# w_in's third block behind the casts, batch 1's globals ahead of w_out, batch 0's gathers ahead of the iotas

## Chip, cores and metric

The kernel runs on 1 core of one Trainium2 chip. The metric is the time of one execution in device microseconds, as the median of several runs; lower is better. Before the change it is 374.94 us, the median of 3 runs (374.66 to 376.61).

The core's engines work side by side, each through its own list of instructions in order: PE (matrix multiply), DVE (vector), ACT (activation functions), POOL (general, and the issuer of every transfer that casts or gathers) and SP (issuer of the plain transfers and of the transposing ones). They wait for one another by semaphores.

## What is computed

Attention with a band of 32 positions to each side and 8 global positions, for 8 batches of 8 heads, 576 positions and 64 values per head; then, on the 4608 tokens of 512 values, two matrix products with a periodic activation between them. Inputs and output are float32.

```
scores = scale * q @ k.T          # scale = 1/sqrt(64)
mask   = |i - j| <= 32  or  i is global  or  j is global
scores = where(mask, scores, -1e9)
attn   = softmax(scores)
x      = (attn @ v)  as [tokens, heads * 64]
h = x @ w_in                      # 512 x 2048
g = h + sin(alpha * h)**2 / (alpha + 1e-9)
out = g @ w_out                   # 2048 x 512
```

## The kernel before

The order of work on every engine is written out by hand. Attention of batch b+1 runs together with the second product (`gemm2`) of batch b, and then `gemm1` of batch b+1 follows; `gemm2`'s matmuls are dealt out by `fill(n)`, n at a time, between the others. All of PE's work is one list in program order, so a matmul that waits holds back all that stand behind it.

**Attention.** For each batch the keys lie in KX, the queries in QX, the values in VX (two buffers of each, by b % 2), each cut into blocks of 48 positions with the 8 global ones beside them, so that one 128-wide product covers both. A head pair hp (four per batch) has three groups of `scores` (L741), each followed on ACT by an exp (L749) and on DVE by a product with MASK (L752). `products` (L783) then multiply E by VX (key 0) and by OB, for the sums (key 1); for batch 1 and later those of head pair hp - 1 are done in the turn of hp. Logarithm, exponential and product give the normalised rows xT (L809 to L815).

**gemm1(b).** 16 groups nt of 8 matmuls each (L990), into PSUM banks named n, r, d and o (`order`): o is the pair zo, which is also gemm2's and, once, that of `turn_kq`. Each group is read by ACT (sine, L1020), squared on ACT or DVE (L1024, L1026), and put together on DVE into H (L1028). Groups 0 to 3 use columns of w_in's first block, 4 to 7 of the second, 8 to 11 of the third, 12 to 15 of the fourth. During groups 10 to 13 of batch 0, DVE also places half of batch 1's keys and queries (`place`, L349 and L356).

**Transfers.** POOL issues `load_w_in` (four blocks, L410), `load_w_out` (four blocks, L416), `load_v` (L393, four transfers per head pair), `cast_qk` (L330, a batch's k and q cast to bf16 in DRAM), and the indirect gathers of batch 0's global rows (L553). SP issues `turn_qk` (L339, the transposing loads kt and qt of cast k and q), `gather` (L488, eight transfers each: the global rows of all batches, gk, gq and gv) and `load_vg` (L402, the global rows of v into VX). After its three memsets for batch 1's buffers POOL waits, by a copy into `seen` (L1118), until kt has landed; only behind that stand w_in's third and fourth block, the values of batch 1's head pairs 0 and 1, and, on SP behind qt, `gather(v, gv)`.

**Globals.** `turn_kq` (L697) turns gk and gq by eight PE transposes into zo[1] and copies them on DVE to kTg and qTg. `cast_globals_v` (L695) casts gv to VGb on POOL. `place_globals(b)` (L366) copies kTg and qTg on POOL into KX and QX of a batch: eight copies of 64x96 and two of 128x112. Batch 0's own globals come earlier, from the three gathers at L553 (g0k, g0q, VG0).

**The start.** POOL issues batch 0's k and q (four loads, L443), makes the identity and six iotas (qrel four times, qpos, jrow), then the three gathers. ACT clears QX and half of VX, squares qrel (L557), clears the rest of VX. DVE makes `band` and MASK from qrel, then `far` from qpos and the global positions (L638 to L666), which it puts into MASK. PE turns keys and queries (`turn_part`, L590); ACT places the first keys (`place_part`, L606), DVE the first queries (L611), and ACT the globals of batch 0 (L621, L630).

In `gemm1`, at group 11 of batch 0, the order before is:

```
            if b == 0 and nt == 11:
                turn_kq()
            if b == 0 and nt == 11:

                load_w_out()
                cast_globals_v()
                place_globals(1)
                load_v(1, (2, 3))
                load_vg(1)
```

Of the kernel before, what the change touches and what calls it, by code (L numbers as in the profile page):

```python
# [247 lines left out]
def kernel(  # L248
# [117 lines left out]
    def place_globals(b):  # L366

        for hp in range(NHP):
            for t in range(2):
                rows = slice(t * D, (t + 1) * D)  # L370
                nc.gpsimd.tensor_copy(
                    out=KX[b % 2][rows, hp, :, t * D + KT : t * D + KT + NG],
                    in_=kTg[rows, hp, None, :, b].to_broadcast([D, NT12, NG]),
                )
# [73 lines left out]
    qrel = setup.tile([P, 2, 2, WCOL // 2], DT.float32, name="qrel")  # L448
    for par, left in ((0, PAD), (1, 40)):
        nc.gpsimd.iota(qrel[:, par, :, 0:left], pattern=[[1, 2], [2, left]], base=-WIN,  # L450
                       channel_multiplier=0, allow_small_or_imprecise_dtypes=True)
        nc.gpsimd.iota(qrel[:, par, :, left:60], pattern=[[1, 2], [2, 60 - left]],
                       base=2 * left - 40, channel_multiplier=0, allow_small_or_imprecise_dtypes=True)
    qpos = setup.tile([P, NT12, 2, 24], DT.float32, name="qpos")
    nc.gpsimd.iota(qpos[:], pattern=[[KT, NT12], [1, 2], [2, 24]], base=0, channel_multiplier=0,
                   allow_small_or_imprecise_dtypes=True)
    jrow = setup.tile([P, NG], DT.float32, name="jrow")
    nc.gpsimd.iota(jrow[:], pattern=[[1, NG]], base=0, channel_multiplier=0,
                   allow_small_or_imprecise_dtypes=True)


# [71 lines left out]
    nc.vector.tensor_copy(out=grow[:], in_=rowf[0 : NG * B, 4:5])  # L533
    nc.vector.memset(kflat[:, half : 2 * half], 0.0)
# [15 lines left out]
    g0 = {}  # L550
    for name, src in (("k", k), ("q", q), ("v", v)):
        g0[name] = VG0 if name == "v" else setup.tile([NG * B, D], DT.bfloat16, name="g0" + name)
        nc.gpsimd.indirect_dma_start(  # L553
            out=g0[name][:], out_offset=None, in_=src[0].rearrange("h s d -> (h s) d"),
            in_offset=bass.IndirectOffsetOnAxis(ap=grow[:, 0:1], axis=0),
        )
    nc.scalar.activation(out=qrel[:], in_=qrel[:], func=AF.Square, bias=kpos[:, 0:1], scale=-1.0)  # L557
    clear(vflat[:, half : 2 * half])
# [5 lines left out]
    cast_qk(1)  # L564
    load_vg(0)
# [62 lines left out]
    def place_global_queries(t, copy):  # L628
# [7 lines left out]

    gpf = setup.tile([P, 1], DT.float32, name="gpf")
    nc.vector.tensor_copy(out=gpf[:], in_=gp64[:].bitcast(DT.int32)[:, 0:1])  # L638
    nc.scalar.activation(out=qpos[:], in_=qpos[:], func=AF.Square, bias=gpf[:, 0:1], scale=-1.0)
# [6 lines left out]
    later = setup.tile([P, NG], DT.float32, name="later")  # L646
    nc.vector.tensor_scalar(
        out=later[:], in0=jrow[:], scalar1=pm, scalar2=float(-KT), op0=ALU.subtract, op1=ALU.is_ge
    )
# [3 lines left out]
    nc.vector.scalar_tensor_tensor(  # L653
        out=cond[:, 2:3], in0=pm, scalar=float(KT + NG - 1), in1=cond[:, 1:2], op0=ALU.is_le, op1=ALU.mult
    )
    nc.vector.tensor_tensor(out=fone[:], in0=fone[:], in1=cond[:, 2:3], op=ALU.mult)

    far = setup.tile([P, NT12, 2, 24], DT.bfloat16, name="far")
    nc.vector.tensor_scalar(
        out=far[:], in0=qpos[:], scalar1=float(WIN * WIN) + 0.5,  # L660
        scalar2=fone[:, 0:1], op0=ALU.is_gt, op1=ALU.mult,
    )
    farv = far[:].rearrange("p (t e) x c -> p t e x c", e=2)
    for e, c0 in ((0, 20), (1, 16)):
        own = M2[:, :, e].rearrange("p t (x c) -> p t x c", x=2)[:, :, :, c0 : c0 + 24]
        nc.vector.tensor_tensor(out=own, in0=own, in1=farv[:, :, e], op=ALU.max)  # L666

    turn_part(1, 0, views([zn[:, n, :] for n in range(2)]))
    for n in range(2):
        place_part(1, 0, n, act)  # L670
# [542 lines left out]
```

## Time and profile before

| | us |
|---|---|
| median of 3 runs | 374.94 |
| the profiled execution | 374.3 |
| its span, first to last instruction | 372.6 |
| PE busy in the span | 338.7 |
| ACT busy | 293.9 |
| DVE busy | 282.8 |
| POOL busy | 138.3 |
| attention of batch 0: first scores on PE | 15.48 |
| gemm1 of batch 0: first matmul | 31.97 |
| attention of batch 1: first scores | 54.05 |
| gemm1 of batch 1: first matmul | 71.67 |

The profile is of one execution; its times are measured from the span's start. In a timeline each line has the start, the time taken (several like instructions merged, "xN"), the engine, the line of the kernel, the operation, output and inputs by their names in the program, shapes and types, and in brackets the idle time of the engine just before it with what ended it. The name H stands for several tiles that lie in one buffer, among them gk, gq and gv. Transfers issued by POOL run in one queue (q0, software), those of SP in another (q1, hardware); both are carried out by the same 16 DMA engines. The time of a transfer "to landing" counts from its issue.

### The profile page before, as it was taken

The numbers are of one execution on the slowest core, as the hardware profiler recorded it, in microseconds if no ns is written. First come the engines' busy times: TensorE is split into PE (matmuls) and PEld (weight loads), VectorE is DVE, ScalarE is ACT, GpSimd is POOL, SyncE is SP. The second block draws the span as 40 slices with busy tenths as digits, with TensorE's granted clock in tenths as the row PEclk, the third lists the DMA queues.
The fourth block names the chain that finished last, engine by engine and source line by source line (L and its number), as shares of the span: only waits on it lengthen the run. The fifth ranks groups of instructions, "written<-read, shape, count | busy, mean of one in ns | idle before, by whom it ended". The sixth has DMA issues, their size and how long they took to land. (4 is left out here: it accounts for less than half of the span.)

```text
span 372.6 us, 8428 instructions
## 1 busy us (share of the span) xinstructions
PE 338.7 (91%) x3040; PEld 228.7 (61%) x3040; DVE 282.8 (76%) x621; ACT 293.9 (79%) x566; POOL 138.3 (37%) x246
## 2 busy tenths in 40 slices
PE   1678769999998999999999999999999999994993
PEld 1567546766576766767676756776667666551441
DVE  6777897598878787888788878888878776888240
ACT  7799897888878788878888888888888988788110
POOL 7894596669844604470357016700000000000001
PEclk9999998999999999999999999999999999998998
DMA  6999999999999586966498517626100000101211
GB/s 120 115 158 209 152 155 184 147 186 187 154 210 213 35 157 100 160 98 90 68 175 119 84 58 67 65 46 143 30 28 30 23 35 31 31 0 35 75 61 52
DMA packets 103579, 38.07 MB, mean 102 GB/s; under 512 B 94138, under 2 KB 98250, under 8 KB 103082
## 3 DMA queue, kind: packets, MB, share of 16 engines
q0 software_dynamic: 56640, 18.56, 43.9%
q1 hardware_dynamic: 46890, 18.89, 24.4%
q8 instruction: 26, 0.43, 0.5%
q14 instruction: 23, 0.19, 0.2%
HBM read 37.15 MB, written 17.83 MB: 148 GB/s over the span
## 5 line engine op out<-in xcount | busy, mean ns | idle before, releaser
L1047 PE MATMUL zo<-w_out,H 128*128 128x512 bf16 x576 | 155.4, 382 | 4.9 <-ACT osb L1053 4.9
L990 PEld LDWEIGHTS <-w_in 128*128 128x128 bf16 x1024 | 98.6, 98 | 47.7 <-issue 10.3
L393 POOL DMA_DIRECT2D VX<-in_v_dram x128 | 83.2, 662 | 92.7 <-PE zd L783 60.9
L1047 PEld LDWEIGHTS <-H 128*128 128x128 bf16 x576 | 52.6, 98 | 43.4 <-issue 7.2
L749 ACT ACTIVATE E<-ring 128x480 bf16<-128x480 f32 x96 | 54.3, 568 | 21.8 <-PE ring L741 21.4
L752 DVE TENSOR_TENSOR E<-E,MASK 128x480 bf16<-128x480 bf16 x96 | 35.9, 404 | 16.8 <-ACT E L749 15.5
L1075 POOL DMA_INDIRECT out_dram<-osb,grow x1 | 1.0, 998 | 126.9 <-DVEq L1181 126.9
L1028 DVE SCALAR_TENSOR_TENSOR H<-s,recipT,zn 128x576 bf16<-128x576 bf16 x47 | 38.2, 813 | 10.0 <-ACT s L1024 6.2
L1024 ACT ACTIVATE s<-sb 128x576 bf16<-128x576 bf16 (+1 forms) x62 | 42.7, 689 | 2.0
L1020 ACT ACTIVATE sb<-zn,alphaT 128x576 bf16<-128x576 f32 (+1 forms) x47 | 34.8, 740 | 11.6 <-PE zn L990 11.6
L741 PE MATMUL ring<-QX,KX 128*128 128x120 bf16 x384 | 37.8, 224 | 6.3 <-ACT E L749 3.3
L741 PEld LDWEIGHTS <-KX 128*128 128x128 bf16 x384 | 28.8, 101 | 21.9 <-issue 10.3
L1028 DVE SCALAR_TENSOR_TENSOR H<-s,recipT,zd 128x576 bf16<-128x576 bf16 x39 | 31.7, 813 | 6.6 <-ACT s L1024 4.7
L1028 DVE SCALAR_TENSOR_TENSOR H<-s,recipT,zr 128x576 bf16<-128x576 bf16 x39 | 31.7, 812 | 4.6 <-ACT s L1024 2.5
L1053 ACT COPY osb<-zo 128x512 f32<-128x512 f32 x36 | 20.7, 578 | 17.8 <-PE zo L1047 14.8
L1026 DVE TENSOR_TENSOR s<-sb 128x576 bf16<-128x576 bf16 (+1 forms) x66 | 30.6, 464 | 5.2 <-ACT sb L1020 4.9
L1020 ACT ACTIVATE sb<-zd,alphaT 128x576 bf16<-128x576 f32 (+1 forms) x39 | 28.9, 741 | 7.2 <-PE zd L990 5.6
L1020 ACT ACTIVATE sb<-zr,alphaT 128x576 bf16<-128x576 f32 (+1 forms) x39 | 28.9, 741 | 5.6 <-PE zr L990 5.6
L783 PEld LDWEIGHTS <-VX 128*128 128x128 bf16 x448 | 26.3, 99 | 9.3 <-issue 3.1
L990 PE MATMUL zn<-xT,w_in 128*128 128x288 bf16 x184 | 26.9, 286 | 4.2 <-DMA w_in<-in_moe_w_in_dram 2.0
L990 PE MATMUL zn<-xlast,w_in 128*128 128x288 bf16 (+1 forms) x192 | 28.8, 289 | 0.3
L783 PE MATMUL zn<-E,VX 128*128 128x120 bf16 (+2 forms) x336 | 26.6, 210 | 1.0 <-DVE xlast L815 0.9
(159 smaller groups left out, 488.3 us busy)
## 6 DMA issues: line engine op xcount, KB each, us to landing
VX<-in_v_dram POOLq DMA_DIRECT2D x128, 36.0 KB, 5.6
kd<-in_k_dram POOLq DMA_DIRECT2D x7, 576.0 KB, 7.2
qd<-in_q_dram POOLq DMA_DIRECT2D x7, 576.0 KB, 9.2
w_in<-in_moe_w_in_dram POOLq DMA_DIRECT2D x4, 512.0 KB, 6.5
w_out<-in_moe_w_out_dram POOLq DMA_DIRECT2D x4, 512.0 KB, 8.9
out_dram<-osb SPq DMA_DIRECT2D x8, 256.0 KB
out_dram<-osb SPq DMA_DIRECT2D x8, 224.0 KB
out_dram<-osb SPq DMA_DIRECT2D x8, 192.0 KB
```

Source lines behind the costliest of these rows:

```text
L393: nc.gpsimd.dma_start(out=VX[b % 2][r : r + 24, hp, :, t * D : t * D + D], in_=v[b, 2 * hp + t].rearrange("(i a y) d -> y a i d", a=24, y= ...
L741: nc.tensor.matmul(out=ps[:, e * WCOL : (e + 1) * WCOL], lhsT=kx[:, hp, i, :], rhs=qx[:, hp, :, s0 : s0 + 60], start=True, stop=True, skip ...
L749: nc.scalar.activation(out=Eg, in_=ps[:, 0 : 4 * WCOL], func=AF.Exp, scale=scale, accum_out=EA[:, n : n + 1])
L752: nc.vector.tensor_tensor(out=Eg, in0=Eg, in1=MASK[:, 4 * g : 4 * g + 4, :].rearrange("p i c -> p (i c)"), op=ALU.mult,)
L783: nc.tensor.matmul(out=out_t[:, half, :, a - half * CUT : z - half * CUT], lhsT=OB[:] if key else VXb[:, hp, i, :], rhs=E[:, i, :, a - s0 ...
L990: nc.tensor.matmul(out=h[e][:, 0:W], lhsT=lhsT, rhs=xT[:, c, e, 0:W], start=(c == 0), stop=(c == CT - 1), skip_group_check=True,)
L1020: nc.scalar.activation(out=sb[:, es, 0:W], in_=h[:, :, 0:W], func=AF.Sin, scale=alphaT[:, nt : nt + 1])
L1024: nc.scalar.activation(out=s2[:, :, 0:W], in_=sb[:, :, 0:W], func=AF.Square)
L1026: nc.vector.tensor_tensor(out=s2[:, :, 0:W], in0=sb[:, :, 0:W], in1=sb[:, :, 0:W], op=ALU.mult)
L1028: nc.vector.scalar_tensor_tensor(out=H2[:, nt, r0 : r0 + S].rearrange("p (e c) -> p e c", e=2)[:, es], in0=s2[:, es, 0:HALF], scalar=recip ...
L1047: nc.tensor.matmul(out=ops[:], lhsT=H2[:, nt, blk * P : (blk + 1) * P], rhs=w_out[:, nt, :], start=(nt == 0), stop=(nt == NT - 1),)
L1053: nc.scalar.copy(out=osb[:], in_=ops[:])
```

## The change

Four things are moved, and one is done in fewer instructions:

- the gathers of batch 0's global k and q rows stand ahead of the six iotas on POOL; that of v behind them. On ACT the rest of VX is cleared before the square of qrel;
- the steps that make `far` and put it into MASK stand behind the first query copies on DVE, and the square of qpos behind ACT's copies of batch 0's globals; `turn_part(1, 0)` and ACT's key copies stand ahead of them in the program;
- w_in's third block is issued right behind `cast_qk(1)`, ahead of POOL's memsets and of the `seen` copy; the fourth stays where it was;
- at group 10 of batch 0 instead of 11 come `turn_kq`, the cast of VGb and `place_globals(1)`, then `load_w_out`, which stood ahead of the cast, then the values of head pairs 2 and 3;
- `place_globals(1)` copies all four head pairs in one instruction for each half (two of 64x384 instead of eight of 64x96).

```diff
--- before.py
+++ after.py
@@ -365,12 +365,14 @@
 
     def place_globals(b):
 
-        for hp in range(NHP):
+        step = NHP if b == 1 else 1
+        for hp in range(0, NHP, step):
+            hps = slice(hp, hp + step)
             for t in range(2):
                 rows = slice(t * D, (t + 1) * D)
                 nc.gpsimd.tensor_copy(
-                    out=KX[b % 2][rows, hp, :, t * D + KT : t * D + KT + NG],
-                    in_=kTg[rows, hp, None, :, b].to_broadcast([D, NT12, NG]),
+                    out=KX[b % 2][rows, hps, :, t * D + KT : t * D + KT + NG],
+                    in_=kTg[rows, hps, None, :, b].to_broadcast([D, step, NT12, NG]),
                 )
         for y in range(2):
             nc.gpsimd.tensor_copy(
@@ -445,20 +447,6 @@
                 in_=src[0, HH * half : HH * half + HH].rearrange("h (i r) d -> (h i) (r d)", r=KT),
             )
     make_identity(nc, identb[:])
-    qrel = setup.tile([P, 2, 2, WCOL // 2], DT.float32, name="qrel")
-    for par, left in ((0, PAD), (1, 40)):
-        nc.gpsimd.iota(qrel[:, par, :, 0:left], pattern=[[1, 2], [2, left]], base=-WIN,
-                       channel_multiplier=0, allow_small_or_imprecise_dtypes=True)
-        nc.gpsimd.iota(qrel[:, par, :, left:60], pattern=[[1, 2], [2, 60 - left]],
-                       base=2 * left - 40, channel_multiplier=0, allow_small_or_imprecise_dtypes=True)
-    qpos = setup.tile([P, NT12, 2, 24], DT.float32, name="qpos")
-    nc.gpsimd.iota(qpos[:], pattern=[[KT, NT12], [1, 2], [2, 24]], base=0, channel_multiplier=0,
-                   allow_small_or_imprecise_dtypes=True)
-    jrow = setup.tile([P, NG], DT.float32, name="jrow")
-    nc.gpsimd.iota(jrow[:], pattern=[[1, NG]], base=0, channel_multiplier=0,
-                   allow_small_or_imprecise_dtypes=True)
-
-
     g64 = setup.tile([NG * B, 1], DT.int64, name="g64")
     gidx8 = setup.tile([P, NG], DT.int64, name="gidx8")
     gp64 = setup.tile([P, 1], DT.int64, name="gp64")
@@ -531,6 +519,30 @@
         out=rowf[0 : NG * B, 4:5], in0=rowf[0 : NG * B, 0:1], scalar=float(S), in1=rowf[0 : NG * B, 3:4], op0=ALU.mult, op1=ALU.add
     )
     nc.vector.tensor_copy(out=grow[:], in_=rowf[0 : NG * B, 4:5])
+
+    g0 = {}
+
+    def gather_first(name, src):
+        g0[name] = VG0 if name == "v" else setup.tile([NG * B, D], DT.bfloat16, name="g0" + name)
+        nc.gpsimd.indirect_dma_start(
+            out=g0[name][:], out_offset=None, in_=src[0].rearrange("h s d -> (h s) d"),
+            in_offset=bass.IndirectOffsetOnAxis(ap=grow[:, 0:1], axis=0),
+        )
+
+    gather_first("k", k)
+    gather_first("q", q)
+    qrel = setup.tile([P, 2, 2, WCOL // 2], DT.float32, name="qrel")
+    for par, left in ((0, PAD), (1, 40)):
+        nc.gpsimd.iota(qrel[:, par, :, 0:left], pattern=[[1, 2], [2, left]], base=-WIN,
+                       channel_multiplier=0, allow_small_or_imprecise_dtypes=True)
+        nc.gpsimd.iota(qrel[:, par, :, left:60], pattern=[[1, 2], [2, 60 - left]],
+                       base=2 * left - 40, channel_multiplier=0, allow_small_or_imprecise_dtypes=True)
+    qpos = setup.tile([P, NT12, 2, 24], DT.float32, name="qpos")
+    nc.gpsimd.iota(qpos[:], pattern=[[KT, NT12], [1, 2], [2, 24]], base=0, channel_multiplier=0,
+                   allow_small_or_imprecise_dtypes=True)
+    jrow = setup.tile([P, NG], DT.float32, name="jrow")
+    nc.gpsimd.iota(jrow[:], pattern=[[1, NG]], base=0, channel_multiplier=0,
+                   allow_small_or_imprecise_dtypes=True)
     nc.vector.memset(kflat[:, half : 2 * half], 0.0)
     nc.vector.memset(tiny[:], TINY)
     nc.vector.memset(OB[:], 0.0)
@@ -547,21 +559,16 @@
                 start=True, stop=True, skip_group_check=True,
             )
 
-    g0 = {}
-    for name, src in (("k", k), ("q", q), ("v", v)):
-        g0[name] = VG0 if name == "v" else setup.tile([NG * B, D], DT.bfloat16, name="g0" + name)
-        nc.gpsimd.indirect_dma_start(
-            out=g0[name][:], out_offset=None, in_=src[0].rearrange("h s d -> (h s) d"),
-            in_offset=bass.IndirectOffsetOnAxis(ap=grow[:, 0:1], axis=0),
-        )
+    gather_first("v", v)
+    clear(vflat[:, half : 2 * half])
     nc.scalar.activation(out=qrel[:], in_=qrel[:], func=AF.Square, bias=kpos[:, 0:1], scale=-1.0)
-    clear(vflat[:, half : 2 * half])
     load_v(0, (0,))
     load_w_in((0,))
     load_v(0, (1, 2))
     load_w_in((1,))
     load_v(0, (3,))
     cast_qk(1)
+    load_w_in((2,))
     load_vg(0)
     gather(q, gq)
 
@@ -634,40 +641,29 @@
                 ].to_broadcast([D, NHP, 7, 4]),
             )
 
+    turn_part(1, 0, views([zn[:, n, :] for n in range(2)]))
+    for n in range(2):
+        place_part(1, 0, n, act)
+    later = setup.tile([P, NG], DT.float32, name="later")
+    nc.vector.tensor_scalar(
+        out=later[:], in0=jrow[:], scalar1=pm, scalar2=float(-KT), op0=ALU.subtract, op1=ALU.is_ge
+    )
+    nc.vector.scalar_tensor_tensor(
+        out=cond[:, 2:3], in0=pm, scalar=float(KT + NG - 1), in1=cond[:, 1:2], op0=ALU.is_le, op1=ALU.mult
+    )
     gpf = setup.tile([P, 1], DT.float32, name="gpf")
     nc.vector.tensor_copy(out=gpf[:], in_=gp64[:].bitcast(DT.int32)[:, 0:1])
-    nc.scalar.activation(out=qpos[:], in_=qpos[:], func=AF.Square, bias=gpf[:, 0:1], scale=-1.0)
     gf = setup.tile([P, NG], DT.float32, name="gf")
     nc.vector.tensor_copy(out=gf[:], in_=gidx8[:].bitcast(DT.int32)[:, 0::2])
     first = setup.tile([P, NG], DT.float32, name="first")
     nc.vector.tensor_scalar(
         out=first[:], in0=gf[:], scalar1=gpf[:, 0:1], scalar2=None, op0=ALU.not_equal
     )
-    later = setup.tile([P, NG], DT.float32, name="later")
-    nc.vector.tensor_scalar(
-        out=later[:], in0=jrow[:], scalar1=pm, scalar2=float(-KT), op0=ALU.subtract, op1=ALU.is_ge
-    )
     nc.vector.tensor_tensor(out=first[:], in0=first[:], in1=later[:], op=ALU.max)
     fone = setup.tile([P, 1], DT.float32, name="fone")
     nc.vector.tensor_reduce(out=fone[:], in_=first[:], axis=AX.X, op=ALU.min)
-    nc.vector.scalar_tensor_tensor(
-        out=cond[:, 2:3], in0=pm, scalar=float(KT + NG - 1), in1=cond[:, 1:2], op0=ALU.is_le, op1=ALU.mult
-    )
     nc.vector.tensor_tensor(out=fone[:], in0=fone[:], in1=cond[:, 2:3], op=ALU.mult)
 
-    far = setup.tile([P, NT12, 2, 24], DT.bfloat16, name="far")
-    nc.vector.tensor_scalar(
-        out=far[:], in0=qpos[:], scalar1=float(WIN * WIN) + 0.5,
-        scalar2=fone[:, 0:1], op0=ALU.is_gt, op1=ALU.mult,
-    )
-    farv = far[:].rearrange("p (t e) x c -> p t e x c", e=2)
-    for e, c0 in ((0, 20), (1, 16)):
-        own = M2[:, :, e].rearrange("p t (x c) -> p t x c", x=2)[:, :, :, c0 : c0 + 24]
-        nc.vector.tensor_tensor(out=own, in0=own, in1=farv[:, :, e], op=ALU.max)
-
-    turn_part(1, 0, views([zn[:, n, :] for n in range(2)]))
-    for n in range(2):
-        place_part(1, 0, n, act)
     turn_part(0, 0, views([zd[:, n, :] for n in range(2)]))
     for n in range(2):
         place_part(0, 0, n, dve)
@@ -680,7 +676,17 @@
     for t in range(2):
         place_global_keys(t, act)
         place_global_queries(t, act)
+    nc.scalar.activation(out=qpos[:], in_=qpos[:], func=AF.Square, bias=gpf[:, 0:1], scale=-1.0)
     act(out=alphaT[:], in_=both[:, 0:NT])
+    far = setup.tile([P, NT12, 2, 24], DT.bfloat16, name="far")
+    nc.vector.tensor_scalar(
+        out=far[:], in0=qpos[:], scalar1=float(WIN * WIN) + 0.5,
+        scalar2=fone[:, 0:1], op0=ALU.is_gt, op1=ALU.mult,
+    )
+    farv = far[:].rearrange("p (t e) x c -> p t e x c", e=2)
+    for e, c0 in ((0, 20), (1, 16)):
+        own = M2[:, :, e].rearrange("p t (x c) -> p t x c", x=2)[:, :, :, c0 : c0 + 24]
+        nc.vector.tensor_tensor(out=own, in0=own, in1=farv[:, :, e], op=ALU.max)
     turn_part(0, 1, views([z[:] for z in zo]))
     turn_part(1, 1, views([zn[:, n, :] for n in range(2)]))
     def second_half():
@@ -999,13 +1005,11 @@
                     place(b + 1, which, t, y, nc.vector.tensor_copy, slice(0, NHP if b else 2))
             if b == 1 and nt in (3, 4):
                 square_x(0, nt - 3)
-            if b == 0 and nt == 11:
+            if b == 0 and nt == 10:
                 turn_kq()
-            if b == 0 and nt == 11:
-
-                load_w_out()
                 cast_globals_v()
                 place_globals(1)
+                load_w_out()
                 load_v(1, (2, 3))
                 load_vg(1)
             if nt == 0:
@@ -1116,7 +1120,7 @@
                     nc.gpsimd.memset(KX[1][:].bitcast(DT.int32), 0)
                     turn_qk(1)
                     nc.gpsimd.tensor_copy(out=seen[:], in_=turned[1][1][0:1, 0:1])
-                    load_w_in((2, 3))
+                    load_w_in((3,))
                     load_v(1, (0, 1))
                     gather(v, gv)
                 return
```

## The prediction

> **Where the end is set.** I read the page first: engine shares, then the span in 40 slices of 9.3 us.
>
> ```profile
> PE 338.7 (91%) x3040; PEld 228.7 (61%) x3040; DVE 282.8 (76%) x621; ACT 293.9 (79%) x566; POOL 138.3 (37%) x246
> PE   1678769999998999999999999999999999994993
> POOL 7894596669844604470357016700000000000001
> ```
>
> PE is full from slice 6 on, where it runs a list written in program order. The change touches nothing after 72 us. So what reaches the end is how much sooner batch 1's gemm1 starts on PE (71.67 us in the trace), unless a later transfer is too late for it. Next I read the timelines of PE, ACT, DVE and POOL over 0 to 72 us, for what ended each idle time. The bracket is the idle time in us before an instruction and its releaser.
>
> ```profile
> 15.48 0.96 PE L741 MATMUL ring<-QX,KX 128*128 128x120 bf16 x8 [0.98 <-DVE QX L611]
> 42.22 1.15 PE L990 MATMUL zn<-xT,w_in 128*128 128x288 bf16 x8 [1.95 <-DMA w_in<-in_moe_w_in_dram]
> 54.05 0.37 PE L741 MATMUL ring<-QX,KX 128*128 128x120 bf16 x4 [1.96 <-POOL QX L376]
> 65.94 1.02 PE L1047 MATMUL zo<-w_out,H 128*128 128x512 bf16 x4
> 66.80 0.36 PE L783 MATMUL zn<-E,VX 128*128 128x88 bf16 x4
> 43.41 0.74 ACT L1020 ACTIVATE sb<-zn,alphaT 128x576 bf16<-128x576 f32 x1 [1.21 <-PE zn L990]
> 53.39 1.28 ACT L725 ACT_TABLE_LOAD   x1
> 11.61 3.73 DVE L611 COPY QX<-zd 64x288 bf16<-64x288 bf16 x8
> 44.18 0.46 DVE L1026 TENSOR_TENSOR s<-sb 128x576 bf16<-128x576 bf16 x1 [0.97 <-ACT sb L1020]
> 45.88 0.81 DVE L1028 SCALAR_TENSOR_TENSOR H<-s,recipT,zr 128x576 bf16<-128x576 bf16 x1 [0.32 <-ACT s L1024]
> ```
>
> PE has three stops that the change is about: query placement, w_in's third block, batch 1's globals. Behind the second, DVE has no idle time worth naming from 46 to 61 us, so DVE's loss is the price there, not PE's.
>
> POOL issues the casting and V transfers. Its waits fit one rule: each waits for the landing of the transfer eight before it (at 19.16 the eighth V behind w_in's first block, at 61.06 the eighth behind w_out's last).
>
> ```profile
> 36.06 1.55 POOL L410 DMA_DIRECT2D w_in<-in_moe_w_in_dram  x2
> 46.53 3.04 POOL L416 DMA_DIRECT2D w_out<-in_moe_w_out_dram  x4
> 50.12 3.13 POOL L371 COPY KX<-kTg 64x96 bf16<-64x96 bf16 x8
> 53.31 0.69 POOL L376 COPY QX<-qTg 128x112 bf16<-128x112 bf16 x2
> 61.06 0.64 POOL L393 DMA_DIRECT2D VX<-in_v_dram  x1 [2.34 <-DMA w_out<-in_moe_w_out_dram]
> ```
>
> **Start: 0.9 us.** The gathers of k and q move ahead of the six iotas. POOL's work only changes places (iotas 4.29 to 5.69, three gathers at 1.28 each), so the first V still goes out at 9.3. The gather of k lands 5.9 us after its issue (11.75), yet the last q load, issued at 3.23, lands at 8.4 later (11.6), in the same queue just ahead. An earlier issue gains nothing (0) to 1.4 us; I take 0, by the neighbour in the queue. The later iotas put the square of qrel at about 7.4 instead of 4.93 and the MASK copy's end at 9.05 instead of 7.34; DVE then waited for gidx until 9.28 anyway, so this cover hides most. Then, on DVE: gpf, gf, first, max, reduce and product end at about 10.4. far (0.52) and the two MASK maxima (0.53) now stand behind the query copies, which start at 10.4 instead of 11.61 and end at 14.1. ACT's global copies end at 14.06 as before, so scores start at about 14.2 instead of 15.48: 1.28. Part is given back: qpos (0.77) now stands on ACT after them, far and MASK wait for it (14.85 to 15.9), recipT 0.42, the first masked E at 16.4 instead of 16.83; but DVE's second query copies go from 18.58 to 17.8 and ACT's key copies from 18.01 to 16.8. Between DVE's 0.8 and ACT's 1.2 I take **0.9**, bounds 0 and 1.3.
>
> **w_in's third block: 1.3 us.** It is issued behind the casts at 24.2 (POOL 0.79, hidden: after its memsets POOL stood from 30.7 to 35.83). In half-us windows of the transfer view the casts' last packets run to 31.3, then POOL's queue is empty until 37.5. A block takes 3.3 us there (the two landed at 42.2 and 45.45), so it lands by 36, before nt 8 asks at 39.4. PE's 1.95 goes; DVE gets 0.97 + 0.32 = **1.3** (bounds 0 and 1.95). The fourth block, now alone behind the `seen` wait, lands 6.1 after 36.1, at 42.2, needed at about 44.9.
>
> **The block at nt 10: 0.** turn_kq comes one group sooner, but needs zo[1], freed by DVE at 43.2 - 0.9 = 42.3: PE's nt 10 slips by 0.7, ACT with it. ACT's lead covers it: E's first exp ended at 55.25, DVE reached it at 56.01 (0.76); without this cover it costs 0.7. The two casts (0.83 on DVE) only swap places, and PE's 0.52 wait for them before nt 14 goes.
>
> **Globals before w_out: 0 gained, 0.3 lost.** The 1.96 stop is hidden already: ACT loads its table until 54.67 and exp starts at 54.68. Merged copies: a 96-element copy takes 0.35, a 1x1 copy 0.18, so 0.18 + 384 x 1.75 ns = 0.85 each, two for 1.7 instead of 3.13 (bounds 1.1, by the 512-element VGb cast's 0.63, and 3.1, no gain). But POOL now stands at the VGb cast until gv is there, and with it everything behind: globals, w_out, V, casts; SP's load_vg(1), which waits for VGb, comes sooner instead. gv's packets, sent from SP at 36.13 to 43.0, flowed until 48.0, behind w_in's blocks and V. With one block (3.3) out of their way: 44.7, landing 45.7; bounds 44.5 and 50. w_out then goes out at T = 45.7 + 0.63 + 1.7 + 0.69 = 48.7 instead of 46.53: 2.2 late. While POOL copied (50.5 to 53.5) w_out moved 80 packets per half us, later 97; that cover gives 0.5 back, so 1.7.
>
> What is queued behind w_out: V of head pairs 2 and 3, then batch 2's casts.
>
> ```profile
> VX<-in_v_dram POOLq DMA_DIRECT2D x1, 36.0 KB, 7.3
> q0 software_dynamic: 1000, 1.00, 118.7%
> q1 hardware_dynamic: 450, 0.05, 14.3%
> ```
>
> The first line is the first of these V transfers, 7.3 us from issue to landing though it moves 36 KB: it stands behind w_out. Windows around the next issues put the fourth's landing at 63.2; hp 2's products need it at 66.80. All earlier by 2.2, they ask at 64.6; it lands at 63.2 + 1.7 = 64.9: **0.3** late, after which V's landing sets the path. w_out's last block, 60.8 + 1.7 = 62.5, is needed at 63.7. Batch 2's casts land 68.3 + 1.7; their copies on DVE start at 88.57, so that is hidden.
>
> Sum: -0.9 - 1.3 + 0.3 = **-1.9 us**. The profiled execution took 374.3 (span 372.6 and 1.7 around it), so 372.4; the median of the runs is 0.64 higher, 374.94, so **373.0**.
>
> **Rivals.**
> V's landing takes the whole gain. If gv comes no sooner than it did (48.0), T = 51.0, w_out 4.5 - 0.5 = 4.0 late, V at 67.2 against 66.80: +0.4, 375.3. For it: nothing between the fourth V and PE gives, and gv's rate moved little with what ran beside it. Against: POOL itself leaves the queue empty while it waits. 0.20.
>
> Slower: w_in's block slows the transposes. kt and qt run at 32 to 37.5, kt lands at 35.83 and releases `seen`, and gv's issues stand behind qt on SP. The last two lines above, w_out beside load_vg from 54.5 to 59.5, show 1000 packets on 16 engines against 450 on 8: equal turns per engine. In a block's 512 packets a transpose gets as many of its 2304, instead of some 1000 per us: 2 us later, gv to 50, T = 53.0, V at 63.2 + 6 = 69.2: +2.4, 377.3. It decides (beyond 0.5%) from T = 52.5. Against: the fourth block then runs alone, so gv meets one block less, and POOL's own wait empties the queue for it. 0.15. The Trainium skill, "DMA: Bandwidth & Descriptors", Queues, rings and completion order, says each engine goes round the queue rows that have work, a packet at a time; the trace agrees (62.5 against 56 per engine), and by it the block's early place is not free.
>
> Full gain: V in time, and the clock holds. PE's granted clock is 0.83, 0.50 and 0.81 in 54 to 60, after the 1.96 stop; L741's four matmuls take 0.56 to 0.61 instead of 0.37. With scores up to 1.2 sooner, exp's 1.24 wait at 59.54 shrinks and DVE's wait for R (0.45) goes: -2.2 - 0.5 = -2.7, 372.2. 0.17. The Trainium skill, "TensorE: Matmul & The Clock Gate", Part 1, has a free-running window of about 3.4 us; the slow stretch of about 3.6 us agrees. By it the phase decides, so 0 to 0.5.
>
> The start gives nothing (the later mask steps fall on DVE's chain): -1.0, 373.9. 0.06.
>
> **Numbers.** Forecast 0.42 (own range 372.3 to 373.9). 0.5% of 374.94 is 1.9 us, what a measurement of this kernel tells from no change: faster is below 373.07, slower above 376.8. Faster: 0.17 of the full gain, 0.27 of the forecast, 0.03 of the others, 0.47. Slower: 0.15 and 0.03 of the first rival, 0.18. Same 0.35. Range: 371.5 to 376.2, to hold 8 in 10.
>
> **What would show it.** Scores near 14.2; no wait for w_in at nt 8; VGb cast near 45.7, first w_out issue near 48.7; PE's wait at hp 2's products ended by V. Wrong if gemm1 of batch 1 starts after 71.67, or if a wait appears behind 72 us.

## The result, and the profile after

The changed kernel takes 379.82 us, the median of 6 runs (377.98 to 380.71), where the kernel before takes 375.62, the median of its 6 runs in the same comparison: a ratio of 1.0118, 95% interval 1.0077 to 1.0159. It is slower by 1.2%; 373.0 was forecast. The profiled execution took 377.98 us with a span of 376.3, 3.7 more than before. It is the fastest of the six, so the trace accounts for 3.7 of the 4.2 us between the medians.

The page of the changed kernel: busy time, then PE and POOL in 40 slices.

```profile
PE 340.3 (90%) x3040; PEld 229.1 (61%) x3040; DVE 283.4 (75%) x621; ACT 293.4 (78%) x566; POOL 137.5 (37%) x240
PE   2679967799999899999999999999999999994993
POOL 8992683678874612570176006800000000000001
```

PE is busy for 1.6 us more and DVE for 0.6, ACT and POOL for less. Slices 6 and 7 of PE (counted from 0; 56.4 to 75.3 us), full before, are at seven tenths. The timeline of PE in the changed kernel shows the stops:

```profile
14.92 0.96 PE L747 MATMUL ring<-QX,KX 128*128 128x120 bf16 x8 [0.47 <-ACT alphaT L680]
40.25 1.14 PE L996 MATMUL zn<-xT,w_in 128*128 128x288 bf16 x8
43.12 0.86 PE L709 MATMUL zo<-idf,H 64*128 64x64 f32 x8 [0.75 <-DVE H L1032]
52.02 0.37 PE L747 MATMUL ring<-QX,KX 128*128 128x120 bf16 x4 [1.47 <-DVE QX L349]
66.92 1.02 PE L1051 MATMUL zo<-w_out,H 128*128 128x512 bf16 x4 [2.52 <-DMA w_out<-in_moe_w_out_dram]
68.94 0.36 PE L789 MATMUL zn<-E,VX 128*128 128x88 bf16 x4 [0.99 <-DMA VX<-in_v_dram]
71.29 2.17 PE L1051 MATMUL zo<-w_out,H 128*128 128x512 bf16 x6
73.29 0.79 PE L789 MATMUL zr<-E,OB 128*128 128x88 bf16 x14
75.41 0.90 PE L996 MATMUL zn<-xlast,w_in 128*128 128x288 bf16 x6
```

Two of these steps in the kernel before:

```profile
68.26 1.46 PE L1047 MATMUL zo<-w_out,H 128*128 128x512 bf16 x6
69.56 0.79 PE L783 MATMUL zr<-E,OB 128*128 128x88 bf16 x14
```

Read from the top: the wait for w_in at group 8 is gone (40.25, no bracket), and batch 1's scores start at 52.02, 2.03 sooner than before. Then two stops appear that were not there: 2.52 us for w_out, and 0.99 for the values of head pair 2. The six matmuls at 71.29 take 2.17 us, before 1.46. Batch 1's gemm1 starts at 75.41, before 71.67. Later batches keep that: the last gemm1 starts at 315.2, before 311.5.

POOL's timeline says why w_out is late, and SP's stands below it:

```profile
37.52 0.18 POOL L1122 COPY seen<-kt 1x1 bf16<-1x1 bf16 x1 [7.05 <-DMA kt<-kd]
44.33 0.65 POOL L395 DMA_DIRECT2D VX<-in_v_dram  x1 [1.27 <-DMA w_in<-in_moe_w_in_dram]
48.50 0.60 POOL L701 CAST VGb<-H 64x512 bf16<-64x512 f32 x1 [3.52 <-DMA H<-in_v_dram]
49.06 1.81 POOL L373 COPY KX<-kTg 64x384 bf16<-64x384 bf16 x2
50.93 0.77 POOL L378 COPY QX<-qTg 128x112 bf16<-128x112 bf16 x2
51.66 3.02 POOL L418 DMA_DIRECT2D w_out<-in_moe_w_out_dram  x4
```

```profile
29.32 6.00 SPq L339 DMA_TRANSPOSE kt<-kd  x1
35.42 2.14 SPq L339 DMA_TRANSPOSE qt<-qd  x1
37.76 6.76 SPq L476 DMA_DIRECT2D H<-in_v_dram  x8
```

The kernel before, for comparison (SP's kt and gv, POOL's cast, which waits for nothing):

```profile
30.39 3.20 SPq L339 DMA_TRANSPOSE kt<-kd  x1
36.13 6.87 SPq L488 DMA_DIRECT2D H<-in_v_dram  x8
49.56 0.63 POOL L695 CAST VGb<-H 64x512 bf16<-64x512 f32 x1
```

POOL is done with its values at 45.0 and stands for 3.52 us at VGb's cast, until gv is there at 48.5. The globals' copies follow, and w_out's first issue comes at 51.66, before at 46.53. Meanwhile the queues run dry. The windows of the changed kernel, then three of the kernel before (length, then busy time of PE, PEld, DVE, ACT and POOL with counts, PE's granted clock, DMA share, GB/s):

```profile
46.00:48.00 2.00, 1.57 (x14) 1.12 (x12) 1.63 (x4) 1.97 (x4) 0.00 (x0) 1.00 0.27 20
48.00:50.00 2.00, 2.00 (x18) 1.61 (x17) 1.96 (x4) 1.94 (x4) 1.49 (x2) 1.00 0.01 4
50.00:52.00 2.00, 0.56 (x5) 0.21 (x4) 1.89 (x5) 1.97 (x5) 1.91 (x4) 1.00 0.13 18
68.00:70.00 2.00, 1.06 (x18) 1.09 (x19) 0.00 (x0) 0.00 (x0) 1.90 (x4) 0.83 1.44 176
70.00:72.00 2.00, 2.00 (x20) 1.58 (x18) 0.41 (x1) 1.14 (x3) 2.00 (x4) 0.50 0.71 138
72.00:74.00 2.00, 2.00 (x20) 1.20 (x19) 1.11 (x3) 1.51 (x4) 0.91 (x2) 0.82 0.90 184
```

```profile
46.00:48.00 2.00, 2.00 (x16) 1.48 (x16) 1.96 (x4) 1.94 (x4) 1.85 (x3) 1.00 0.95 73
48.00:50.00 2.00, 1.30 (x10) 0.87 (x9) 1.92 (x5) 1.97 (x4) 2.00 (x4) 1.00 1.06 132
50.00:52.00 2.00, 1.90 (x15) 1.36 (x14) 1.92 (x5) 1.97 (x4) 1.82 (x6) 1.00 1.17 165
```

From 46 to 52 they move 20, 4 and 18 GB/s, before 73, 132 and 165. In 70 to 72 PE runs at half its clock: that is the longer time of the matmuls at 71.29. With the parts at half clock in the windows beside it (0.83 and 0.82 are means) the slow stretch lasts 0.7 + 2.0 + 0.7 = 3.4 us.

The loss can be added up on PE from the end of the w_out stop. Without its stop the matmul at 66.92 would have come at 64.40, where before it came at 65.94: 1.54 ahead. Then +2.52 (w_out), +0.99 (values of head pair 2) and 0.17 because the four matmuls ahead of the second stop run to their end (1.02) before it, where before the products began 0.16 ahead of their end: head pair 2's products at 68.94, before 66.80, 2.14 late. The two stops are one wait, for the values: they landed at 68.9, so without the stop for w_out PE would have stood for them until then all the same. From there to the zr products it takes 4.35 us (to 73.29), before 2.76: +1.59 for the clock. 2.14 + 1.59 = 3.73, which is the 75.41 against 71.67 (3.74).

### The profile page after: what moved, and what is told of

It reads as the page before. It is cut to its first block, busy times and chain, and to the rows that moved or that the text cites. A ratio compares the mean times of both kernels' runs of the same rounds, so it can differ in the third digit from the quotient of the medians.

```text
span 376.3 us, 8422 instructions
## 1 busy us (share of the span) xinstructions
PE 340.3 (90%) x3040; PEld 229.1 (61%) x3040; DVE 283.4 (75%) x621; ACT 293.4 (78%) x566; POOL 137.5 (37%) x240
## 5 line engine op out<-in xcount | busy, mean ns | idle before, releaser
L755 ACT ACTIVATE E<-ring 128x480 bf16<-128x480 f32 x96 | 54.2, 567 | 24.8 <-PE ring L747 24.5
```

Source lines behind the costliest of these rows:

```text
L755: nc.scalar.activation(out=Eg, in_=ps[:, 0 : 4 * WCOL], func=AF.Exp, scale=scale, accum_out=EA[:, n : n + 1])
```

## The experiments

Theory A: what costs is w_out's place behind VGb's cast, which stands until gv lands. Theory B: w_in's third block, beside the transposes, makes kt, qt and so gv late (the slower rival). Diffs are against the changed kernel unless "before" is said; some are given in outline.

What one trace can tell is bounded by two things that differ between executions, also where the code is the same. At the start, batch 0's first scores come at 15.48 to 16.16 us in the three traces with the start as before (before, e4, e5), at 14.89 to 15.55 in the eleven with the new start, and at 14.52 to 14.80 in the four that also have alphaT's copy first; gemm1 of batch 0 comes at 31.97 to 33.25, 31.72 to 33.02 and 31.37 to 31.67. At the end, from the start of the last gemm1, nine traces take 60.8 to 61.2 us, and in them PE's first stretch at half clock after 340 us lasts about 3.4 us; the other nine take 61.6 to 62.2, and there it lasts about 6.8. Two executions that are level at the last gemm1 can so end some 1 us apart, and smaller differences are left to the medians.

**1. w_out ahead of the cast again** (e1), all else as changed.

```
             if b == 0 and nt == 10:
                 turn_kq()
+                load_w_out()
                 cast_globals_v()
                 place_globals(1)
-                load_w_out()
```

> The changed kernel with load_w_out ahead of the VGb cast again (still at nt 10). Theory A (the price is w_out's late issue: POOL stands at the VGb cast until gv is there, and w_out and the V transfers of head pairs 2 and 3 are 5 us late): first w_out issue near 45 us, no wait of PE for w_out or V, batch 1's gemm1 from about 69.5 us, and 1.5 to 2.5 us faster than before. Theory B (w_in's third block beside the transposes is the price, by a kt that lands 1.7 us late): still slower than before by 1 us or more.

Measured: 375.01 us, 0.9997 of before (0.9964 to 1.0029). Its POOL and PE:

```profile
47.29 3.11 POOL L418 DMA_DIRECT2D w_out<-in_moe_w_out_dram  x4 [1.13 <-DMA VX<-in_v_dram]
50.39 0.62 POOL L701 CAST VGb<-H 64x512 bf16<-64x512 f32 x1
53.47 0.37 PE L747 MATMUL ring<-QX,KX 128*128 128x120 bf16 x4 [2.62 <-POOL QX L378]
58.39 0.36 PE L789 MATMUL zn<-E,VX 128*128 128x88 bf16 x4 [1.65 <-DMA VX<-VGb]
```

One line moved gives the whole loss back. Neither w_out nor head pair 2's values stop PE any more. The 1.5 to 2.5 us that were expected on top didn't come: PE now stands 2.62 us for the globals and 1.65 for VX from VGb.

**2. w_in's third block back behind `seen`** (e2).

```
     cast_qk(1)
-    load_w_in((2,))
     load_vg(0)
...
-                    load_w_in((3,))
+                    load_w_in((2, 3))
```

> The changed kernel with w_in's third block back behind the seen copy; the globals stay ahead of w_out. Theory A: gv lands at about 48 us as before the change, first w_out issue near 51, PE waits for w_out and V again, and the wait for w_in of up to 2 us is back: 2 to 5 us slower than before. Theory B: kt lands near 35.8 again, and the time is that of before or up to 1 us better.

Measured: 378.4, 1.0075 of before (1.0042 to 1.0108). kt is back at 36.28, and gv is as late as it was:

```profile
48.71 0.60 POOL L700 CAST VGb<-H 64x512 bf16<-64x512 f32 x1 [1.77 <-DMA H<-in_v_dram]
```

w_out goes out at 51.73 (51.66 with the block early). Theory B falls: gv and w_out are as late without the early block.

**3. One part alone.** Before with the start's edits (e3); before with the order and the merged copies at group 10 (e4); before with w_in's third block behind the casts (e5); before with start and block (e6).

```
 e4, against before (the merged copies are left out here):
-            if b == 0 and nt == 11:
+            if b == 0 and nt == 10:
                 turn_kq()
-                load_w_out()
                 cast_globals_v()
                 place_globals(1)
+                load_w_out()
```

> The kernel before with the edits of the start alone (gathers ahead of the iotas, mask steps behind the query copies). By the trace of the changed kernel, where batch 0's gemm1 began 0.16 us sooner, both theories expect no change that can be told: within 0.5 us of before. A third theory (the start costs something later) expects over 1 us slower.

> The kernel before with the block at nt 10 alone (globals ahead of w_out, merged copies); w_in's blocks and the start as before. Theory A: 2 to 5 us slower than before, PE waiting for w_out and for V around 65 to 70 us. Theory B: no slower than before.

> The kernel before with w_in's third block behind the casts alone. Theory A: the wait for w_in at nt 8 goes and DVE gains about 1.3 us; kt lands near 37.5 us, which costs nothing: 0.7 to 2 us faster than before. Theory B: kt, the fourth block and gv are 1.7 us late, and the time is that of before or over 1 us slower.

> The kernel before with the start's edits and w_in's third block moved, the block at nt 11 as before (w_out first, eight copies). Theory A: as the changed kernel with w_out first, 1.5 to 2.5 us faster than before; the wait of PE for batch 1's globals is back in the trace (the QX copy on POOL) and costs up to 1 us of it.

Measured against before: start 0.9987 (0.9955 to 1.0019), globals 1.0103 (1.0026 to 1.0179), block 1.0003 (0.9977 to 1.0029), start and block 0.9989 (0.9966 to 1.0012). What stands at group 10 makes the loss alone, and since e1 keeps the merged copies and the group without loss, it is the order that makes it. PE has the same two stops:

```profile
49.50 0.61 POOL L697 CAST VGb<-H 64x512 bf16<-64x512 f32 x1 [2.54 <-DMA H<-in_v_dram]
52.75 3.02 POOL L418 DMA_DIRECT2D w_out<-in_moe_w_out_dram  x4
68.35 1.02 PE L1047 MATMUL zo<-w_out,H 128*128 128x512 bf16 x4 [1.30 <-DMA w_out<-in_moe_w_out_dram]
70.27 0.53 PE L785 MATMUL zn<-E,VX 128*128 128x88 bf16 x4 [0.89 <-DMA VX<-in_v_dram]
```

And the two gains of the forecast give nothing that can be told, together (e6, where 1.5 to 2.5 us were expected) or alone. In the run with the block alone PE no longer waits for w_in, and the next stop takes it:

```profile
54.05 0.56 PE L742 MATMUL ring<-QX,KX 128*128 128x120 bf16 x4 [2.36 <-POOL QX L376]
```

The wait for the globals is 2.36 instead of 1.96, and the scores start at 54.05 as before; that they agree to the hundredth is chance, since this execution began gemm1 of batch 0 1.28 us later. With the block beside the transposes kt lands later (`seen` at 38.67 against 35.83), and POOL's globals end when they did. Batch 1's gemm1 starts at 71.22, 0.45 sooner than before, in this one trace; at the end nothing of it can be told.

**4. Narrower: only VGb's cast behind w_out** (e8), and the globals first, then the cast, then w_out (e11).

```
 e8:                          e11:
 turn_kq()                    turn_kq()
 place_globals(1)             place_globals(1)
 load_w_out()                 cast_globals_v()
 cast_globals_v()             load_w_out()
```

> The changed kernel with the VGb cast behind load_w_out, the globals still ahead of it. Theory A, in its narrow form (not the globals ahead of w_out but the cast's wait for gv is the price): first w_out issue near 48.7 us, V of head pair 2 lands near 65.5, a wait of PE for V of at most 1 us, and the time within 1.5 us of before on the faster side. If w_out is late already by the globals alone: V at 67 us or later and the time no better than before.

> The changed kernel with the globals first, then the VGb cast, then w_out: POOL does the globals while gv is on its way. First w_out issue near 49.1 us instead of 51.66, load_vg from 49.2. Theory A: V of head pair 2 lands near 66, PE's waits for w_out and V sum to under 1.5 us instead of 3.5, and PE's clock is not halved behind them: 2 to 3.5 us faster than the changed kernel, within 1.5 us of before. Rival (globals ahead of w_out is itself the price): as slow as the changed kernel.

Measured: e8 377.84, 1.0093 (1.0063 to 1.0123); e11 376.69, 1.0042 (1.0027 to 1.0058). In e8 w_out goes out at 48.52 and the scores start at 51.39, the soonest of all, yet it stays slow. Its PE:

```profile
59.78 0.53 PE L789 MATMUL zn<-E,VX 128*128 128x88 bf16 x4 [2.89 <-DMA VX<-VGb]
```

Now the global rows of the values are the late ones: SP's `load_vg(1)` waits for the cast (51.55) and lands behind w_out. PE's clock, 0.87 in 54 to 56 and so halved already ahead of this stop, stays at 0.50 until 64. In e11 the cast comes at 50.30 and the wait is 1.31; it ends 1.65 us over the kernel before, where up to 1.5 was expected. So the cast, the globals and w_out all want POOL at the same time, and each order makes another one late. That V of VGb takes w_out's place was not in theory A as it stood then.

**5. w_out in halves** (e9): two blocks ahead of the cast, two behind the globals (`load_w_out` takes the blocks as an argument); e7 and e10 add ACT's alphaT copy ahead of the square of qpos, to e1 and e9.

```
 e9:                              e7, e10, ahead of first scores:
+                load_w_out((0, 1))     +    act(out=alphaT[:], in_=both[:, 0:NT])
                 cast_globals_v()            nc.scalar.activation(out=qpos[:], ...)
                 place_globals(1)       -    act(out=alphaT[:], in_=both[:, 0:NT])
-                load_w_out()
+                load_w_out((2, 3))
```

> The changed kernel with load_w_out ahead of the VGb cast, and ACT's copy of alphaT ahead of the square of qpos. In the changed kernel the first scores waited for the alphaT copy (14.92 us), since the ring takes over the PSUM bank that alphaT is read from. If that is the wait that took the start's gain, scores begin near 14.3 us and batch 0's gemm1 0.3 to 0.7 us sooner than 31.81; if the start is held by the half-rate clock of PE up to 24.5 us, gemm1 begins at 31.5 to 31.9 all the same.

> The changed kernel with load_w_out split: the first two blocks ahead of the VGb cast, the other two behind the globals. Theory A (POOL's queue stands empty while POOL waits for gv, and everything behind is late): first w_out issue near 45 us, globals done near 51.7, w_out's last block landed near 62, V of head pair 2 near 64.5; no wait of PE for w_out or V above 0.5 us, batch 1's gemm1 near 70 us, and 1 to 2 us faster than before. Rival (the transfers as a whole bound the stretch up to 72 us, in whatever order): a wait for V or VGb takes the place of those removed, and the time is that of before.

> As the one before, with ACT's copy of alphaT ahead of the square of qpos: scores of batch 0 near 14.6 instead of 14.9 us as in the earlier run with that edit. Theory A: up to 0.4 us faster than the one before, 1.3 to 2.3 us faster than the kernel before. Rival: no change that can be told from before.

Measured against before: e7 1.0009 (0.9993 to 1.0025), e9 0.9987 (0.9971 to 1.0003), e10 0.9976 (0.9957 to 0.9995; 374.28 against 375.04). e10 is 0.24% below the kernel before; the interval just clears 1, and it is the lowest of sixteen variants, so part of it may be luck. The 1 us or more that e9 and e10 were expected to gain didn't come. With alphaT first the scores of batch 0 start at 14.52 to 14.80 in four traces, ahead of all eleven without it (14.89 to 15.55), so the copy of alphaT did hold them. At the end e7 can't tell it from nothing, and e10 is 0.3 us below e9 with intervals that overlap.

**6. The clock** (e12): 8 more matmuls into zo[1], whose sums aren't kept, in the place of the w_out stop.

```
+                if b == 1 and hp == 3 and g == 1:
+                    warm(zo[1], 8)
                 fill(per_scores[hp][g])
```

> The changed kernel with eight extra matmuls on ones (into a bank whose sums aren't kept) just ahead of the stop for w_out's last block; the work of the kernel is unchanged. If the stop costs a second time by halving PE's clock (69 to 73 us, 0.60 instead of 0.37 us for four matmuls), the clock stays at full rate and batch 1's gemm1 begins at 73.6 to 74.2 instead of 75.4 us, 1 to 1.6 us faster than the changed kernel. If the clock costs nothing there (ACT and DVE set the pace), gemm1 begins at 75.2 us or later.

Measured: 380.47, 1.0141 (1.0105 to 1.0177). Its windows in the same columns:

```profile
70.00:72.00 2.00, 1.17 (x27) 1.20 (x27) 0.00 (x0) 0.00 (x0) 1.88 (x4) 1.00 1.45 171
72.00:74.00 2.00, 2.00 (x26) 1.29 (x23) 0.76 (x3) 1.88 (x4) 2.00 (x4) 1.00 0.75 147
```

The clock stays at 1.00, and from head pair 2's products to zr it takes 2.75 us (4.35 in the changed kernel, 2.76 before): the 1.59 was the clock. That the extra matmuls kept it up isn't shown, because e13 below keeps it without them, behind two stops of much the same length:

```profile
67.32 1.02 PE L1051 MATMUL zo<-w_out,H 128*128 128x512 bf16 x4 [1.98 <-DMA w_out<-in_moe_w_out_dram]
69.04 0.36 PE L789 MATMUL zn<-E,VX 128*128 128x88 bf16 x4 [0.69 <-DMA VX<-in_v_dram]
```

From 69.04 to zr e13 takes 2.76 us, while e4, with shorter stops (1.30 and 0.89), has the clock at 0.51 in 70 to 72 and takes 4.21. e12's total is no better: in this execution gv came only at 50.37, w_out went out at 53.41, and PE had the values at 70.83, so gemm1 of batch 1 began at 75.70 and not at the expected 73.6 to 74.2. What the clock alone is worth at the end stays open: e13 starts gemm1 of batch 1 at 73.91, 1.5 us ahead of the changed kernel, and by that of batch 3 (159.67 against 159.25) the lead is gone, for a reason that wasn't looked for.

**7. Why gv is late** (e13 to e16). e13 has SP ask for gv between the two transposes; e14 and e15 do that to e10, e15 with VGb's cast ahead of w_out's first half; e16 takes batch 1's first eight value transfers from beside gv and puts them behind w_out.

```
 e13, in outline:                      e16, in outline:
     transpose kt                          seen, load_w_in((3,))
+    gather(v, gv)                    -    load_v(1, (0, 1))
     transpose qt                          gather(v, gv)
     seen, load_w_in((3,))                 ...
     load_v(1, (0, 1))                     load_w_out()
-    gather(v, gv)                    +    load_v(1, (0, 1, 2, 3))
```

> The changed kernel, with the eight rows of gv asked for on SP between the transposes of k and q of batch 1 instead of behind both. Theory A (what the changed order costs is POOL standing at VGb's cast until gv lands): the eight issues begin about 2.1 us sooner (35.4 instead of 37.8), so gv lands near 46.2 and VGb's cast begins there instead of at 48.5; w_out's first issue comes near 49.4 instead of 51.66, its stop on TensorE in batch 1 falls from 2.5 us to about 0.3, and the kernel is about 2 to 3 us faster than the changed one (375 to 376 where that is 378 to 379), level with the kernel before or up to 1 us over it. Theory B (the queues are full at that time, and gv lands when they are empty, whatever its place): gv lands at 48 or later all the same, w_out's first issue stays at 51 to 52, the time at 1.008 to 1.012 of before; or the query transpose is late and the place copies of nt 12 wait for qt.

> The version with w_out's first two blocks ahead of VGb's cast, the last two behind the globals, and alphaT's copy first (the best so far), with gv asked for between the two transposes. Theory A: VGb's cast stands right behind the two issues near 49.2 and waits for nothing (0.8 less than without), the globals are placed by 52.4 instead of 53.2, batch 1's scores begin near 52.5 instead of 53.3; 0.3 to 0.8 us faster than without, ratio to before 0.995 to 0.998. Theory B: no change against 0.9976.

> As the run with gv early and w_out in halves, but VGb's cast ahead of w_out's first two blocks. Theory A: VGb's cast near 46.3, w_out's first issue near 47, the globals placed by 51.3, batch 1's scores near 51.5 (1.8 sooner than with w_out first) and V of VGb in time for the first products; gemm1 of batch 1 near 70, ratio to before 0.992 to 0.997. Theory B (gv lands near 48.5 wherever it is asked for): VGb at 48.5, w_out at 49.2, globals at 53.5, no better than 0.9976 and up to 1.002.

> The changed kernel, with the eight issues of V of batch 1's first two head pairs taken from ahead of gv and put behind w_out, so that from 38.5 to 46 gv shares the queues only with the query transpose and w_in's fourth block. Theory B1 (gv is late because it shares the queues with V, 8 x 36 KB, and w_in): gv lands 2 us or more sooner, near 46, and w_out's first issue near 49 instead of 51.66. Theory B2 (gv's eight issues of 128 rows of 256 bytes take their own time at their own rate, about 3 to 4 us behind the last issue at 44.5): gv lands at 48 or later as before, w_out's first issue at 51 or later. In both V of the first two head pairs is late (first landing near 58), so TensorE waits for it near 57 to 60 and the whole is 1.005 to 1.02 of before; the time isn't what this run is for.

Measured: e13 378.61, 1.0094 (1.0062 to 1.0125); e14 376.9, 1.0052 (1.0031 to 1.0074); e15 376.17, 1.0039 (1.002 to 1.0058); e16 385.88, 1.0287 (1.0254 to 1.032). e13's SP and POOL:

```profile
36.22 6.76 SPq L476 DMA_DIRECT2D H<-in_v_dram  x8
48.40 0.60 POOL L701 CAST VGb<-H 64x512 bf16<-64x512 f32 x1 [3.63 <-DMA H<-in_v_dram]
```

Asked for 1.5 us sooner, gv lands when it did: expectation A of these runs failed. The query transpose, pushed behind gv, is late instead; e15's DVE:

```profile
51.01 1.61 DVE L349 COPY QX<-qt 64x576 bf16<-64x576 bf16 x2 [2.55 <-DMA qt<-qd]
```

So e10 stays the best. What holds gv is seen in e16, where no values move beside it: gv's last issue leaves SP at 46.22, and

```profile
47.74 0.60 POOL L701 CAST VGb<-H 64x512 bf16<-64x512 f32 x1 [8.16 <-DMA H<-in_v_dram]
```

that is 1.5 us after the last issue, where in the changed kernel it is 4.0 (44.52 to 48.50) and in e13 5.4. The queue lines of the window 44 to 45 us (packets, MB, share), first of the changed kernel, then of e16:

```profile
q0 software_dynamic: 993, 0.09, 162.7%
q1 hardware_dynamic: 116, 0.03, 15.2%
```

```profile
q1 hardware_dynamic: 268, 0.06, 28.8%
q0 software_dynamic: 15, 0.01, 7.3%
```

With the values beside it gv gets 116 packets where 993 go to POOL's queue, without them 268. By these two traces the traffic beside gv costs it some 2.5 us behind its last issue. Neither expectation of e16 came true as it stood: the cast came 0.8 us sooner and w_out's first issue 0.9 (50.77), where 2 or more, or nothing, were expected, because the issues themselves ended 1.7 later than in the changed kernel. (They are of 64 rows each, not 128.) The rest is the issues, about 0.85 us each on SP, behind both transposes: with the changed kernel's last at 44.52, gv alone would land near 46.0 by this (an estimate from the two traces), still behind the forecast's 45.7. The whole is slow in e16 because the first values are late (PE waits 9.62 for them at 67.66).

## Why the prediction was wrong

**The failed step: gv's landing, "With one block (3.3) out of their way: 44.7, landing 45.7".** It was 48.5. The 3.3 us were subtracted as if gv stood behind w_in's block in one line. It stands in another queue, its pace set by SP's issues and, as e16 shows, by the values' packets beside it, and those were not taken away; kt's longer issue (6.00 on SP instead of 3.20) began its eight issues 1.6 us later besides. Of the bounds, 44.5 and 50, the measured value lies at 3/4 of the way; the first rival's condition (48.0) was what came true, and e4 and e2 show 49.5 and 48.7 with the block in its old place. That 48.0 is where gv's packets ended; the forecast adds 1.0 from there to the landing in its main sum and nothing in the rival.

**The second: the price at that landing.** The rival put T at 51.0 (measured 51.66) and the loss at +0.4; the loss was 3.7. By the forecast's own rule (63.2, plus w_out's lateness of 5.1, less 0.5) the values of head pair 2 come at 67.8 for this T, a loss of 1.0. They landed at 68.9, 5.7 later than before (63.2): the 0.5 that the forecast took off on the way wasn't there, and 0.6 came on top. That is 1.1 more. The halved clock behind the stops (1.59) was in no term of this price, though the profile before showed one behind a stop of 1.96. So of the 5.6 us between the forecast (-1.9) and the trace (+3.7) gv's landing makes 2.9 by the forecast's own rule, the values' later landing 1.1 and the clock 1.6. w_out itself was taken to be in time too ("60.8 + 1.7 = 62.5, is needed at 63.7"); its last block landed at 66.9, 6.1 behind that 60.8, but the wait for the values covers that stop.

The Trainium skill, "TensorE: Matmul & The Clock Gate", Part 1, gives a free-running window of about 3.4 us, and has PE slowed after an idle one; the trace agrees in the length of the slow stretch (3.4 us, from about 69 to 73; the stretch before the change, which the forecast read as 3.6, comes to 3.4 as well from its 0.83, 0.50 and 0.81), while here 2.52 and 0.99 us of idling, neither a whole window, were enough.

**The mechanism of the step was right, its size not.** That POOL would stand at the cast "and with it everything behind" is what happened (3.52 us, where none was seen before); e1, with w_out ahead of the cast, has none of the loss.

**The slower rival** had the right sign (+2.4 us, where the medians differ by 4.2) for the wrong reason. The block does slow the transposes, as it said: SP's issue of kt takes 6.00 instead of 3.20 us, and kt lands 1.7 later (2 forecast); the Trainium skill, "DMA: Bandwidth & Descriptors", Queues, rings and completion order, has each engine go round the queues that have work, and kt's slower issue beside the block is what that would give. But with the block back (e2) gv is no sooner.

**Start, 0.9 forecast:** 0.16 on gemm1 of batch 0 (31.81 against 31.97), which the spread between executions hides (31.72 to 33.02 with the new start), and nothing at the end (e3, 0.9987, 0.9955 to 1.0019). Scores began at 14.92, not 14.2: 0.47 of it is the wait for alphaT's copy, which now stood behind the square of qpos and whose PSUM bank the scores take over. This wait was overlooked. Of the 0.56 gained there 0.16 were left at gemm1; on the way PE's matmuls take half as long again or more until 24.5 (0.56 to 0.60 for four of the scores, later 0.37), and an exp waits 0.59 for them at 25.76.

**w_in's third block, 1.3 forecast:** its wait went as said. On the changed kernel, with globals ahead of w_out, the gain did reach the scores (52.02), and was then lost. By itself it gives nothing that can be told at the end: "The 1.96 stop is hidden already" was wrong in that it becomes the path once the chain ahead of it is shorter; e5 has it at 2.36.

**The rest came as forecast:** `turn_kq` waited 0.75 for DVE (0.7), the query copies 0.77 (0.69), the merged copies 1.81 (1.7), a landing of the fourth block in time, and nothing new behind 76 us.

## What to carry to other kernels

An instruction that waits for a transfer, put ahead of DMA issues on the engine that issues them, delays all of those by its wait: size that wait by the transfer's whole way (when it is issued, what moves beside it, when it lands), not by one competitor taken off. A gain ahead of a stop is only worth what the next stop leaves of it, so each gain should be carried on to the next wait on the path, here POOL's globals. Where several small jobs compete for one issuing engine, splitting the large one (half of w_out ahead, half behind) did at least as well as any order of whole ones (0.9976 and 0.9987 of before, where w_out whole and ahead gave 0.9997 and 1.0009); the intervals overlap.

## What the runs showed of the hardware that was not expected

- A transfer of 64 rows of 256 bytes per issue, eight issues on SP, lands 1.5 us after its last issue when the queues are nearly empty (e16), and 3.4 (e9) to 5.9 (e4) after it with the values moving beside it; 4.0 in the changed kernel.
- The issue of a transpose on SP is not a fixed cost: kt's took 3.20 to 3.85 us in the four traces without a block of w_in beside it (before, e2, e3, e4), and 5.95 to 6.57 in the fourteen with 512 KB of w_in in the other queue.
- Two stops of 2.52 and 0.99 us on PE (1.30 and 0.89 in e4) were followed by about 3.4 us at half the granted clock, at a price of 1.59 us (1.45 in e4). Two of 1.98 and 0.69 (e13), or of 0.87 and 0.90 (e2), were not, so the length of a stop alone doesn't decide it.
- Near the end the slow stretch lasts about 3.4 us in nine traces and about 6.8 in the other nine, and the latter take some 0.4 to 1.4 us longer from the last gemm1 on.
